# Masks of a whole chunk in one VectorE step, the weights' narrowing spread into the first expert, no warming products in the routing's rounds

## The chip, the cores and the metric

The kernel runs on one core of a Trainium2 chip. The metric is the device time of one execution in microseconds (us). TensorE multiplies matrices into PSUM, VectorE and ScalarE work on PSUM and SBUF, GpSimd on SBUF; SyncE's queue (SP) issues most of the loads, ScalarE's queue and GpSimd issue a few others.

## The reference

Three parts follow each other. First a linear attention with a decay for each channel (4 batches, 8 heads, 768 positions, 48 channels a head), then a mixture of 8 experts in which the highest logits of all pairs choose first and each expert takes 384 tokens, then one more block with squared ReLU that all tokens pass:

```python
for t in range(S):
    state = alpha[:, :, t, :, None] * state + einsum('bhd,bhe->bhde', k[:, :, t], v[:, :, t])
    y[:, :, t] = einsum('bhd,bhde->bhe', q[:, :, t], state)
...
logits = x @ w_gate                       # pairs in falling order; a token is taken once, an expert holds N // 8
out[mask] = np.maximum(x[mask] @ w1[e], 0.0) @ w2[e]
...
r = np.maximum(x @ w_in, 0.0)             # d_model 384, d_ff 2048
return (r * r) @ w_out
```

## The kernel before, in words

**Order.** The order of all instructions is written out by hand: each engine works through its own in the order in which the program issues them, and a DMA queue likewise. Generators (prep, narrow, routing, w_load) give out their instructions a step at a time, where the main loop asks with next().

**Attention** (the loop at L664). There are 24 chunks of 128 positions, six to a batch, two to a unit; 8 heads are 4 pairs, and a pair has one head in rows 0 to 47 and the other in rows 64 to 111. prep (L132) scales q and k of a unit: a backward scan of the alphas (f_t, L144), with which GpSimd multiplies k (L146), a forward scan (b_t, L150) from the reciprocal (L148), and the product with q (L152); the last factors are copied to bend (L149). For a chunk s, state_mm (L227) multiplies k and v, and VectorE adds the sum to the state and scales it with bend (L239, L240). scores (L207) makes the products of q and k for both heads of a pair; ScalarE copies them out (L215) and GpSimd sets what lies in the future to zero (L216). k_tok (L219) transposes k. state_bd (L245) copies the state into a block-diagonal tile, with which y_mm (L250) multiplies q, four products of 128 rows (L256), and adds the masked scores times v (L263). x_out (L273) transposes y and writes it to x_d in DRAM from ScalarE's queue; for the last chunks it comes later, in the routing. logits (L283) and logits_t (L291) give the experts' logits.

**Narrowing** (L167). w_in and w_out come as words of 64 bits. They are loaded in 48 pieces of 256 columns into four buffers, three VectorE steps (L179, L182, L185) turn a piece into 32-bit floats (nb), ScalarE rounds that to a high half (L172) and GpSimd subtracts it for the low half (L173). The main loop asks for two pieces in nearly every chunk; all are done before the experts begin.

**Routing of the first expert** (L448, with kk 0, driven at L713 to L720). A threshold is found digit by digit in six rounds. In a round VectorE compares (above, L414), TensorE counts in 24 products (count, L420), VectorE checks the counts (L489), TensorE spreads the result (L492), VectorE forms the next keys (L505). One late x_out stands in each round. warm(n) (L353) issues n products that nothing reads; they stand after the counts (L482), after the spreading (L493) and further on (L498, L564, L614).

**Experts** (the loop at L971). For each of the 8 experts gemm1 and gemm2 do its two layers over 8 slices, gemm3 and gemm4 the last block over 16 slices. Each product of exact operands takes three matmuls with high and low halves (mm3, L839); the low halves are VectorE's (L878, L913). The next expert's routing runs beside it, a step every few products (tick, L851). There, counts of pairs are formed with cross (L423) and summed over rows by GpSimd (L440). w_load0 (L775) brings the first expert's weights in eight pieces: ScalarE makes the high half (L798), VectorE the low half (L799).

## Time and profile before

| | |
|---|---|
| median of 3 runs | 876.11 us (875.86 to 876.43) |
| span of the profiled execution | 874.0 us |
| PE (TensorE) busy | 811.1 us, 93% |
| DVE (VectorE) busy | 558.7 us, 64% |
| ACT (ScalarE) busy | 398.1 us, 46% |
| POOL (GpSimd) busy | 256.1 us, 29% |
| chain that ended last, shares | PE 69%, DVE 16%, issue 10%, POOL 3%, DMA 2% |

Times in the views below are counted from the start of the span. A group of instructions has its line, engine and operation, what it writes and reads, the shapes and the count, then its busy time, the mean of one in ns, and the idle time of its engine before it with what ended it. A matmul of 32-bit floats counts as two instructions. Attention ends at about 192 us, the first expert's products begin at 239 us.

### The profile page before, as it was taken

To read this page: it belongs to the slowest core of one execution; us is meant where nothing else is said; L and a number is where in the kernel's file an instruction comes from. 1 tells how busy PE (TensorE), PEld (TensorE's weight loads), DVE (VectorE), ACT (ScalarE), POOL (GpSimd) and SP (SyncE) were. 2 spreads that over 40 slices of the span, in tenths; PEclk is the share of its full clock that TensorE was granted. 3 is DMA by queue.
4 is the path that set the end of the run, shared out by engine and by line. 5 is a ranking of instruction groups with operands and counts; after the bars stand their busy time and mean duration, and the time that the engine had idled before them with its cause. 6 is when DMAs were issued, how large, how long until landed. Compare 5 with 4: busy or idle time off the path is not lost.

```text
span 874.0 us, 15157 instructions
## 1 busy us (share of the span) xinstructions
PE 811.1 (93%) x5592; PEld 764.8 (87%) x5592; DVE 558.7 (64%) x1528; ACT 398.1 (46%) x904; POOL 256.1 (29%) x248
## 2 busy tenths in 40 slices
PE   4876878789899999999999999999999999999996
PEld 3755767677599999999999999999999999999996
DVE  8999999983576577567656665765666542432211
ACT  3544546451234553464346245534634553662443
POOL 6687887960111131112201221220131210101001
PEclk9988787895799999999999999999999999999998
DMA  8557768521310230131023004201400332210000
GB/s 302 163 149 203 205 189 214 159 79 55 121 61 1 71 111 20 38 101 62 1 73 100 29 1 136 64 1 55 109 37 1 92 104 59 82 37 28 1 1 28
DMA packets 30219, 73.01 MB, mean 84 GB/s; under 512 B 4384, under 2 KB 8224, under 8 KB 30144
## 3 DMA queue, kind: packets, MB, share of 16 engines
q1 hardware_dynamic: 23616, 57.88, 23.2%
q0 software_dynamic: 3072, 9.44, 3.2%
q10 hardware_dynamic: 3456, 4.72, 1.6%
q8 instruction: 44, 0.72, 0.3%
q14 instruction: 31, 0.25, 0.1%
HBM read 62.58 MB, written 9.44 MB: 82 GB/s over the span
## 4 chain that ended last, share of the span: by engine, by line
PE 69%; DVE 16%; issue 10%; POOL 3%; DMA 2%; SPq 0%; ACT 0%; DVEq 0%; POOLq 0%; ACTq 0%
PE hu_p L842 10%; PE hu_p L844 10%; PE hu_p L843 10%; PE acc L926 7%; PE acc L927 7%; PE acc L922 7%; PE acc L842 3%; PE acc L844 3%; PE acc L843 3%; DVE nb L179 3%; DVE nb L182 3%; DVE nb L185 2%; DVE b_t L150 2%; DVE f_t L144 2%; PE rt_p L420 2%
## 5 line engine op out<-in xcount | busy, mean ns | idle before, releaser
L913 DVE TENSOR_TENSOR gl<-rg,gh 128x384 fp32r<-128x384 f32 x127 | 72.2, 568 | 165.5 <-ACT rg L912 164.7
L910 ACT ACTIVATE rg<-hu_p 128x384 f32<-128x384 f32 x128 | 63.0, 492 | 171.5 <-PE hu_p L844 168.1
L842 PE MATMUL hu_p<-zh,wih 128*128 128x384 f32 x384 | 131.5, 342 | 0.0
L926 PE MATMUL acc<-woh,gh 128*128 128x384 f32 x381 | 130.6, 343 | 0.0
L844 PE MATMUL hu_p<-zl,wih 128*128 128x384 f32 x384 | 129.9, 338 | 0.0
L843 PE MATMUL hu_p<-zh,wil 128*128 128x384 f32 x384 | 128.8, 335 | 0.0
L927 PE MATMUL acc<-wol,gh 128*128 128x384 f32 x381 | 128.6, 338 | 0.0
L440 POOL PARTITION_ALL_REDUCE tot<-ex x48 | 52.3, 1089 | 258.3 <-DVE ex L437 258.3
L922 PE MATMUL acc<-woh,gl 128*128 128x384 f32 x381 | 125.8, 337 | 0.0
L877 ACT ACTIVATE hh<-hu_p 128x384 fp32r<-128x384 f32 x64 | 31.5, 492 | 138.7 <-PE hu_p L844 138.7
L878 DVE SCALAR_TENSOR_TENSOR hl<-hu_p,hh 128x384 fp32r<-128x384 f32 x64 | 35.6, 556 | 63.9 <-ACT hh L877 63.8
L844 PEld LDWEIGHTS hu_p<-zl,wih 128*128 128x128 f32 x384 | 72.1, 188 | 1.2
L843 PEld LDWEIGHTS hu_p<-zh,wil 128*128 128x128 f32 x384 | 72.2, 188 | 0.0
L842 PEld LDWEIGHTS hu_p<-zh,wih 128*128 128x128 f32 x384 | 72.1, 188 | 0.0
L926 PEld LDWEIGHTS acc<-woh,gh 128*128 128x128 f32 x381 | 71.5, 188 | 0.1
L927 PEld LDWEIGHTS acc<-wol,gh 128*128 128x128 f32 x381 | 71.6, 188 | 0.0
L922 PEld LDWEIGHTS acc<-woh,gl 128*128 128x128 f32 x381 | 71.2, 188 | 0.0
L623 POOL DMA_INDIRECT xg<-x_d,ix x24 | 26.4, 1102 | 151.7 <-DVE pe L639 94.2
L911 ACT ACTIVATE gh<-rg 128x384 fp32r<-128x384 f32 x127 | 66.7, 525 | 4.0
L842 PE MATMUL hu_p<-xh,w1h 128*128 128x384 f32 x192 | 66.3, 345 | 0.0
L844 PE MATMUL hu_p<-xl,w1h 128*128 128x384 f32 x192 | 65.7, 342 | 0.0
L948 POOL DMA_INDIRECT out_dram<-ob,ix x24 | 23.7, 988 | 143.0 <-DVE ob L946 139.5
(252 smaller groups left out, 1885.6 us busy)
## 6 DMA issues: line engine op xcount, KB each, us to landing
wraw<-in_w_dram SPq DMA_DIRECT2D x62, 384.0 KB, 3.3
raw<-in_w_in_dram SPq DMA_DIRECT2D x24, 256.0 KB, 3.2
raw<-in_w_out_dram SPq DMA_DIRECT2D x24, 256.0 KB, 3.6
vt<-in_v_dram SPq DMA_DIRECT2D x12, 384.0 KB, 5.4
x_d<-xo ACTq DMA_DIRECT2D x24, 192.0 KB, 2.8
a<-in_al_dram SPq DMA_DIRECT2D x18, 193.7 KB, 4.7
k<-in_k_dram SPq DMA_DIRECT2D x18, 192.0 KB, 5.5
q<-in_q_dram SPq DMA_DIRECT2D x18, 192.0 KB, 6.1
```

The lines of the kernel that those rows point to most:

```text
L440: nc.gpsimd.partition_all_reduce(tot[:, :, :J], ex[:, :, :J], 128, bass_isa.ReduceOp.add)
L842: nc.tensor.matmul(dst, wh, xh, start=first, stop=False)
L843: nc.tensor.matmul(dst, wl, xh, start=False, stop=False)
L844: nc.tensor.matmul(dst, wh, xl, start=False, stop=last)
L877: nc.scalar.activation(hh, hp, AF.Relu)
L878: nc.vector.scalar_tensor_tensor(hl, hp, 0.0, hh.bitcast(FT), op0=OP.max, op1=OP.subtract)
L910: nc.scalar.activation(r, up, AF.Relu)
L911: nc.scalar.activation(gh, r, AF.Square)
L913: nc.vector.tensor_tensor(gl, g, gh.bitcast(FT), op=OP.subtract)
L922: nc.tensor.matmul(acc[j], gl[:, j * 128:(j + 1) * 128], woh[:, f, :], start=False, stop=(f == NF2 - 1))
L926: nc.tensor.matmul(acc[j], gh[:, cs], woh[:, f, :], start=(f == 0), stop=False)
L927: nc.tensor.matmul(acc[j], gh[:, cs], wol[:, f, :], start=False, stop=False)
```

## The change

- **Masks.** scores writes both halves into one PSUM tile of two banks, and one VectorE step, a bitwise and with a constant tile of ones and zeros in all bits, masks and copies them. ScalarE's two copies and GpSimd's two selections of a chunk go.
- **State.** VectorE only adds; the scaling by bend is four ScalarE copies with a scale for each row. The block-diagonal copies go: y_mm has eight products of 48 rows, with outputs that swap halves for odd pairs (side), so that y is copied out in two steps, as are the parts of x.
- **Order.** The q product of a unit comes a chunk later, at the start of the next unit's first chunk, and the loads of v, k, alpha and q are issued apart. Loads of later units are one DMA of 112 rows for each tile instead of two of 48. k is not transposed for the last chunk of a batch.
- **Narrowing.** It goes by 16 tiles, each a slice f of w_in and of w_out of 768 columns together, loaded to a place of its own. In attention it has four steps, the subtraction on VectorE among them, and is asked for beside odd chunks only, twice (once in the last four units). Eight more steps stand in the routing's rounds. From then on a tile is done in halves of 384, three steps with the subtraction on GpSimd, beside the first expert. So 5, 2 and 9 tiles.
- **Routing.** The warming products of the rounds go, and three of six after them. For routing(1) the sum over rows is a TensorE product with ones (total) instead of GpSimd's.
- **First expert's weights.** From the fourth piece on the subtraction is GpSimd's.

```diff
...
 NSL = 3
-NWP = 256
-NWB = 4
+NWP = 768
 BIG = 1.5e38
 WD = 3
+NYT = 4
 S0 = NS - 7
-WR, WC, WA, WB, W0 = 3, 2, 3, 2, 3
+WA, WB, W0 = 3, 2, 3
 T0, T1, T2, T3, XF = 5, 4, 5, 5, 11
...
     pt_ = {}
-    def load(u, ends=(CU * HP,)):
+    def load(u, what="akq", ends=(CU * HP,)):
         i = u % NSL
...
         n0 = 0
         for n1 in ends:
...
-                if u < NSL:
-                    nc.sync.dma_start(t[:, x0:x1], src[u, :, x0:x1])
-                else:
-                    for r in (0, 64):
-                        nc.sync.dma_start(t[r:r + D, x0:x1], src[u, r:r + D, x0:x1])
+                R = slice(0, 128 if u < NSL else R2)
+                nc.sync.dma_start(t[R, x0:x1], src[u, R, x0:x1])
             n0 = n1
     def load_v(u):
-        vs[u] = aw.tile([128, CU, DM], FT, name="vt")
+        vs[u] = aw.tile([128, CU, DM], FT, name="vt", bufs=3)
         nc.sync.dma_start(vs[u], v[u])
...
-    bd = [ap_.tile([128, HP, 128], FT, name=f"bd{i}") for i in range(2)]
-    nc.gpsimd.memset(bd[0], 0.0)
-    nc.gpsimd.memset(bd[1], 0.0)
+    mask = ap_.tile([128, 128], I32, name="mask")
+    yts = [ap_.tile([128, HP, 128], FT, name=f"yt{i}") for i in range(NYT)]
+    for t in yts:
+        nc.gpsimd.memset(t, 0.0)
...
+        nc.scalar.activation(bend[i].rearrange("p c a -> p (c a)")[:, cs], f_t[:, cs, 0], AF.Copy)
         nc.vector.reciprocal(d_b[:, cs, 0], f_t[:, cs, 0])
-        nc.vector.tensor_copy(bend[i].rearrange("p c a -> p (c a)")[:, cs], f_t[:, cs, 0])
...
+    raws, wi, wo = {}, {}, {}
+    def narrow_load(n=1):
+        for _ in range(n):
+            f, o = divmod(len(raws), 2)
+            if f >= NF2:
+                return
+            if not o:
+                raw = consts.tile([128, NWP, 2], U32, name=f"raw{f}", tag=f"w{f}")
+                nc.sync.dma_start(raw[:, :DM].rearrange("p (a b) t -> p a (b t)", a=KD),
+                                  w_in[:, :, f * 128:(f + 1) * 128].bitcast(U32))
+            else:
+                raw = raws[f, 0]
+                nc.sync.dma_start(raw[:, DM:].rearrange("p a t -> p (a t)"), w_out[:, f, :].bitcast(U32))
+            raws[f, o] = raw
+    fine = [None]
+    sub_on = [nc.gpsimd]
     def narrow():
...
+        for f in range(NF2):
+            raw = raws[f, 0]
+            if fine[0] is None:
+                ps = [(aw.tile([128, NWP], U32, name="nb"), slice(0, NWP))]
+            else:
+                ps = [(fine[0].tile([128, DM], U32, name="nb", tag="ob", bufs=3), slice(i * DM, (i + 1) * DM))
+                      for i in range(2)]
+            for t, cs in ps:
+                nc.vector.tensor_scalar(t, raw[:, cs, 1], 3, 0x3FFFFFF8, op0=OP.logical_shift_left,
+                                        op1=OP.bitwise_and)
+            yield False
+            for t, cs in ps:
+                nc.vector.scalar_tensor_tensor(t, raw[:, cs, 1], 0xC0000000, t, op0=OP.bitwise_and,
+                                               op1=OP.bitwise_or)
+            yield False
+            for t, cs in ps:
+                nc.vector.scalar_tensor_tensor(t, raw[:, cs, 0], 29, t, op0=OP.logical_shift_right,
+                                               op1=OP.bitwise_or)
+            w = consts.tile([128, 2, NWP], FR, name=f"w{f}", tag=f"w{f}")
+            for t, cs in ps:
+                nc.scalar.activation(w[:, 0, cs], t.bitcast(FT), AF.Copy)
+            if sub_on[0] is nc.vector:
+                yield False
+            for t, cs in ps:
+                sub_on[0].tensor_tensor(w[:, 1, cs], t.bitcast(FT), w[:, 0, cs].bitcast(FT), op=OP.subtract)
+            wi[f] = w[:, :, :DM].rearrange("p h (a b) -> p h a b", a=KD)
+            wo[f] = w[:, :, DM:]
+            yield True
+    def narrow_upto(n):
+        while len(wo) < n:
+            next(nw)
+    sc_p = pp.tile([128, 2, HP, 128], FT, name="sc_p")
+    y_p = pp.tile([128, 2, HP, 128], FT, name="y_p")
...
                 rr = slice(64 * r, 64 * r + D)
-                nc.tensor.matmul(sc_p[r][:, p, :], ks[i][rr, c, p, :], qs[i][rr, c, p, :], start=True, stop=True)
-        for r in range(2):
-            t = aw.tile([128, HP, 128], FT, name=f"am{r}")
-            nc.scalar.activation(t, sc_p[r], AF.Copy)
-            nc.gpsimd.affine_select(t, t, [[0, HP], [1, C]], OP.is_ge, 0.0, base=0, channel_multiplier=-1)
-            am[s, r] = t
+                nc.tensor.matmul(sc_p[:, r, p, :], ks[i][rr, c, p, :], qs[i][rr, c, p, :], start=True, stop=True)
+        t = aw.tile([128, 2 * HP, 128], FT, name="am")
+        nc.vector.tensor_tensor(t.bitcast(I32), sc_p.rearrange("p r a s -> p (r a) s").bitcast(I32),
+                                mask[:, None, :].to_broadcast([128, 2 * HP, 128]), op=OP.bitwise_and)
+        am[s] = t
     def k_tok(s):
...
         _, j, cn = loc(s + 1)
...
+        src = st_p[R, :, :D]
...
+            nc.vector.tensor_tensor(t0[R], src, st[s - 1][R], op=OP.add)
+            src = t0[R]
+        for p in range(HP):
+            nc.scalar.activation(t[R, p, :], src[:, p, :], AF.Copy, scale=bend[j][R, cn, p:p + 1])
         st[s] = t
-    def state_bd(s):
-        z = bd[(s + 1) % 2]
-        for r in range(2):
-            nc.scalar.activation(z[64 * r:64 * r + D, :, 64 * r:64 * r + D], st[s][64 * r:64 * r + D], AF.Copy)
+    def side(p, r):
+        g = r ^ (p & 1)
+        return slice(64 * g, 64 * g + D)
     def y_mm(s):
...
         f = s % NC == 0
...
         if not f:
             for p in range(HP):
-                nc.tensor.matmul(y_p[:, p, :], bd[s % 2][:, p, :], qs[i][:, c, p, :],
-                                 start=(p == 0), stop=False, skip_group_check=True)
+                for r in range(2):
+                    rr = slice(64 * r, 64 * r + D)
+                    nc.tensor.matmul(y_p[side(p, r), r, p // 2, :], st[s - 1][rr, p, :], qs[i][rr, c, p, :],
+                                     start=(p < 2), stop=False, skip_group_check=True)
...
         for p in range(HP):
...
                 h = 2 * p + r
-                nc.tensor.matmul(y_p[64 * r:64 * r + D, p, :], vs[u][:, c, h * D:(h + 1) * D],
-                                 am[s, r][:, p, :], start=(f and p == 0), stop=True, skip_group_check=True)
+                nc.tensor.matmul(y_p[side(p, r), r, p // 2, :], vs[u][:, c, h * D:(h + 1) * D],
+                                 am[s][:, r * HP + p, :], start=(f and p < 2), stop=True, skip_group_check=True)
...
     before = mr.tile([128, 128], FH, name="before")
...
                                  stop=(c == NS - 1))
-        def cross(self, i):
+        def total(self, i):
+            J = self.J[i]
+            tot = rt_p[:, 200:200 + E * J].rearrange("p (e j) -> p e j", e=E)
+            nc.tensor.matmul(tot, ones, ex[:, :, :J], start=True, stop=True)
+            return tot
+        def cross(self, i, pe):
             J = self.J[i]
...
                                     same[:GP, :E, None].to_broadcast([GP, E, J]), op=OP.mult)
+            if pe:
+                return None
             tot = mw.tile([128, E, 16], FT, name="tot", bufs=1)
...
                             key.count(i, a, b)
-                    if i:
-                        warm(WC)
-                    else:
+                    if not i:
                         x_out(next(late))
...
-                        warm(WR)
                     else:
...
                         nc.tensor.matmul(rt_p[:, 200:200 + E], ones[:J], cg[:J], start=True, stop=True)
-                        warm(6)
+                        warm(3)
                 else:
-                    cp = key.cross(i)
+                    cp = key.cross(i, kk == 1)
                     yield TA
+                    if kk == 1:
+                        cp = key.total(i)
                 dp = mr.tile([128, 1], FT, name="dp", bufs=2)
...
+    nc.vector.tensor_scalar(mask, jp, 0.0, -1.0, op0=OP.is_ge, op1=OP.mult)
+    pr = prep(1)
+    next(pr)
     scores(0)
...
+    narrow_load(2)
     load(2)
...
     NE = NS - 4
-    pr = prep(1)
+    load(3, "a")
     next(pr)
-    next(pr)
+    sub_on[0] = nc.vector
     for s in range(NS):
...
         last = s % NC == NC - 1
-        if c == 1:
-            pr = prep(u + 2) if u + 2 < NU else iter(())
         if not last:
             state_mm(s)
+        if c == 0:
+            next(pr, None)
+            pr = prep(u + 2) if u + 2 < NU else iter(())
         next(pr, None)
...
             scores(s + 1)
-        if not last:
-            state_bd(s)
-        if s + 1 < NS:
+        if s + 1 < NS and (s + 1) % NC != NC - 1:
             k_tok(s + 1)
...
             x_out(s - 1)
-        if s + 2 < NS:
-            next(nw, None)
         if c == 1:
-            next(pr, None)
+            for _ in range(2 if u < 8 else 1):
+                next(nw)
         y_mm(s)
...
             key0.above(0, key0.x, 0, NE)
-        if s + 2 >= NS:
-            next(nw, None)
-        logits_t(s - 1 if s == NS - 1 else s - 2)
-        if 0 < s < NS - 1:
+        if s % 2 == 1 and s > 2:
+            logits_t(s - 2)
+        if s % 2 == 0 and s:
+            logits(s - 2)
             logits(s - 1)
-        if c == CU - 1 and u + NSL < NU:
-            load(u + NSL)
-        if c == CU - 1 and u + 2 < NU:
-            load_v(u + 2)
+        if c == 0:
+            if u + 2 < NU:
+                load_v(u + 2)
+            load(u + NSL, "k")
+        else:
+            load(u + NSL + 1, "a")
+            load(u + NSL, "q")
+        if s % 3 < 2:
+            narrow_load()
         if 2 <= s < 4:
...
+    narrow_load(2 * NF2)
     r0 = routing(0)
     next(r0)
-    for _ in nw:
-        pass
-    for _ in range(len(WIDE) - 1):
+    for n in (2, 1, 2, 2, 1):
         next(r0)
         x_out(next(late))
+        for _ in range(n):
+            next(nw)
         next(r0)
+    sub_on[0] = nc.gpsimd
     att.close()
...
             nc.scalar.activation(fh, got[n], AF.Copy)
-            nc.vector.tensor_tensor(fl, got[n], fh.bitcast(FT), op=OP.subtract)
+            (nc.vector if n < 3 else nc.gpsimd).tensor_tensor(fl, got[n], fh.bitcast(FT), op=OP.subtract)
             if len(got) < len(todo):
...
         up = hu()
-        cs = slice(f * 128, (f + 1) * 128)
+        narrow_upto(f + 1)
         for kd in range(KD):
-            mm3(up, (wih[:, kd, cs], wil[:, kd, cs]), (zh[:, kd, :], zl[:, kd, :]), kd == 0, kd == KD - 1)
+            mm3(up, (wi[f][:, 0, kd, :], wi[f][:, 1, kd, :]), (zh[:, kd, :], zl[:, kd, :]), kd == 0, kd == KD - 1)
             tick()
...
                 next(wl[0], None)
+                for _ in range(1 + f % 2):
+                    next(nw, None)
             hn = gemm1(kk, f + 1) if f + 1 < NF1 else None
...
                 h = gemm1(kk + 1, 0)
+            if kk == 0:
+                next(nw, None)
+                next(nw, None)
             if more and f == XF + 3:
...
```

## Rows read from the trace of the kernel before

**Rows 1.** Windows in us: length; PE, PEld, DVE, ACT, POOL busy (count); PEclk; DMA share; GB/s.
```profile
12.00:19.00 7.00, 6.55 (x54) 4.97 (x54) 6.96 (x8) 3.13 (x7) 6.61 (x4) 1.00 1.04 405
120.00:140.00 20.00, 16.46 (x189) 14.18 (x189) 19.93 (x26) 11.05 (x27) 16.97 (x12) 0.79 0.72 196
```

**Rows 2.** The chain that ended last, 140 to 180: start us, us, what.
```profile
143.60 2.21 DVE b_t L150
...
147.58 0.41 DVE nb L179 x2
147.99 0.67 DVE nb L182 x2
...
152.00 2.94 DVE nb L179 x2
...
158.66 2.29 DVE b_t L150
```

**Rows 3.** Groups of VectorE's instructions by shape, 19 to 192: busy us, mean ns, idle.
```profile
L179 DVE TENSOR_SCALAR nb<-raw 128x256 uint32<-128x256 uint32 x47 | 34.0, 761 | 3.6 <-POOL wil L173 2.3 <-POOL wol L173 1.2
L182 DVE SCALAR_TENSOR_TENSOR nb<-raw,nb 128x256 uint32<-128x256 uint32 x46 | 27.6, 639 | 0.0
L185 DVE SCALAR_TENSOR_TENSOR nb<-raw,nb 128x256 uint32<-128x256 uint32 x46 | 26.9, 624 | 0.0
L144 DVE TENSOR_TENSOR_SCAN f_t<-a,d_f 128x1032 f32<-128x1032 f32 x10 | 23.5, 2349 | 0.0
L150 DVE TENSOR_TENSOR_SCAN b_t<-a,d_b 128x1032 f32<-128x1032 f32 x10 | 22.9, 2295 | 0.0
L152 DVE TENSOR_TENSOR q<-q,b_t 128x1024 f32<-128x1024 f32 x11 | 13.6, 1236 | 0.0
...
L240 DVE TENSOR_TENSOR st<-st,be 112x192 f32<-112x192 f32 x16 | 6.6, 412 | 0.6
L239 DVE TENSOR_TENSOR st<-st_p,st 112x192 f32<-112x192 f32 x16 | 5.5, 341 | 0.6 <-PE st_p L231 0.6
```

**Rows 4.** The same of GpSimd.
```profile
L146 POOL TENSOR_TENSOR k<-k,f_t 128x1024 f32<-128x1024 f32 x11 | 27.4, 2491 | 7.0 <-DVE f_t L144 7.0
```

**Rows 5.** The same of ScalarE.
```profile
L248 ACT ACTIVATE bd<-st 48x192 f32<-48x192 f32 x39 | 14.0, 360 | 42.9 <-DVE st L240 29.9 <-DVE st L242 12.7
...
L271 ACT ACTIVATE yt<-y_p 128x512 f32<-128x512 f32 x18 | 10.6, 589 | 4.7 <-PE y_p L263 4.5
```

**Rows 6.** TensorE's timeline at the end of attention: start us, us, engine, line, operation.
```profile
181.03 1.93 PE L256 MATMUL y_p<-q,bd 128*128 128x128 f32 x8
...
184.75 0.56 PE L231 MATMUL st_p<-vt,kt 128*48 128x48 f32 x16
...
189.12 1.16 PE L256 MATMUL st_p<-q,bd 128*128 128x128 f32 x8
```

**Rows 7.** TensorE's timeline in one round of the routing.
```profile
209.68 0.18 PE L492 MATMUL rt_p<-cm,ones 31*128 31x1 f16 x1
...
210.73 0.95 PE L276 MATMUL kt_p<-ident,a 112*128 112x112 f32 x4
211.61 1.76 PE L420 MATMUL rt_p<-oh,m 128*31 128x8 f16 x24
...
214.06 0.18 PE L492 MATMUL rt_p<-cm,ones 31*128 31x1 f16 x1
```

**Rows 8.** VectorE's timeline in that round.
```profile
210.18 0.62 DVE L414 TENSOR_TENSOR m<-xn,jc 128x372 f16<-128x372 f16 x2
...
213.41 0.15 DVE L489 TENSOR_SCALAR_CACHE_REDUCE cg<-rt_p 31x8 f16<-31x8 f32 x1 [2.31 <-PE rt_p L420]
```

**Rows 9.** Windows of the routing and the first expert.
```profile
208.00:212.00 4.00, 4.00 (x31) 2.64 (x31) 1.29 (x7) 0.28 (x1) 0.20 (x1) 0.50 0.16 53
239.00:291.00 52.00, 51.63 (x290) 50.86 (x290) 34.68 (x114) 19.73 (x40) 9.36 (x8) 0.95 0.10 37
```

**Rows 10.** VectorE's groups by shape, 225 to 262.
```profile
L799 DVE TENSOR_TENSOR w1l<-wraw,w1h 128x768 fp32r<-128x768 f32 x3 | 2.9, 955 | 0.0
```

More of the change, by code (lines that the diff above doesn't have):

```diff
@@ L68 @@
     L = consts.tile([128, NS, E], FT)
-    wih = consts.tile([128, KD, F2], FR)
-    wil = consts.tile([128, KD, F2], FR)
-    woh = consts.tile([128, NF2, DM], FR)
-    wol = consts.tile([128, NF2, DM], FR)
     mr = ctx.enter_context(tc.tile_pool(name="route", bufs=1))
@@ L93 @@
     pt_ = {}
-    def load(u, ends=(CU * HP,)):
+    def load(u, what="akq", ends=(CU * HP,)):
         i = u % NSL
+        if u >= NU:
+            return
+        ts = {"a": (as_[i], al), "k": (ks[i].rearrange("p c a s -> p (c a s)"), k),
+              "q": (qs[i].rearrange("p c a s -> p (c a s)"), q)}
         n0 = 0
         for n1 in ends:
-            for t, src in ((as_[i], al), (ks[i].rearrange("p c a s -> p (c a s)"), k),
-                           (qs[i].rearrange("p c a s -> p (c a s)"), q)):
+            for t, src in (ts[w] for w in what):
                 w = src.shape[-1] // (CU * HP)
@@ L128 @@
     load_v(1)
-    nc.sync.dma_start(wgs, wg)
+    for b in range(2):
+        for r in range(2):
+            nc.sync.dma_start(wgs[64 * r:64 * r + 64].rearrange("p (k b) e -> p b k e", b=2)[:, b],
+                              wg[64 * (r ^ b):64 * (r ^ b) + 64].rearrange("p (k b) e -> p b k e", b=2)[:, b])
     nc.gpsimd.iota(jp, pattern=[[1, 128]], base=0, channel_multiplier=-1)
@@ L153, in prep @@
         yield
-    wq = []
-    for h_, l_, src in ((wih, wil, w_in), (woh, wol, w_out)):
-        h2, l2, s2 = (t.rearrange("p a b -> p (a b)") for t in (h_, l_, src))
-        wq += [(h2[:, j:j + NWP], l2[:, j:j + NWP], s2[:, j:j + NWP]) for j in range(0, h2.shape[1], NWP)]
-    raws = []
-    def narrow_load():
-        if len(raws) < len(wq):
-            raw = aw.tile([128, NWP, 2], U32, name="raw", bufs=NWB)
-            nc.sync.dma_start(raw.rearrange("p a b -> p (a b)"), wq[len(raws)][2].bitcast(U32))
-            raws.append(raw)
@@ L195 @@
     xt_p = pp.tile([128, HP, 128], FT, name="xt_p")
-    lg_p = pp.tile([128, 4, 128], FT, name="lg_p")
-    lt_p = pp.tile([128, 4, 128], FT, name="lt_p")
-    y_ps = (y_p, st_p)
+    lg_p = rt_p
+    lt_p = lg_p[:, 256:].rearrange("p (j g) -> p j g", j=2)
     xt_ps = (xt_p, kt_p)
@@ L268, in y_mm @@
         else:
-            yt[s] = aw.tile([128, HP, 128], FT, name="yt")
-        for ps in ([slice(0, HP)] if s < NS - 1 else [slice(0, HP // 2), slice(HP // 2, HP)]):
-            nc.scalar.activation(yt[s][:, ps], y_p[:, ps], AF.Copy)
+            yt[s] = yts[s % NYT]
+        for g in range(2):
+            rr = slice(64 * g, 64 * g + D)
+            nc.scalar.activation(yt[s][rr].rearrange("p (k b) s -> p b k s", b=2),
+                                 y_p[rr, ::(1, -1)[g], :2], AF.Copy)
     def x_out(s):
@@ L277, in x_out @@
         t = aw.tile([128, H, D], FT, name="xo")
-        nc.scalar.activation(t, xt_p.rearrange("p a (r d) -> p (a r) d", r=2)[:, :, :D], AF.Copy)
+        for b in range(2):
+            nc.scalar.activation(t.rearrange("p (k b r) d -> p b k r d", b=2, r=2)[:, b],
+                                 xt_p.rearrange("p (k b) (r d) -> p b k r d", b=2, r=2)[:, b, :, ::(1, -1)[b], :D],
+                                 AF.Copy)
         nc.scalar.dma_start(x_d[s * C:(s + 1) * C, :], t.rearrange("p h d -> p (h d)"))
@@ L648 @@
             pass
-    for t in (y_p, st_p, lg_p):
-        nc.scalar.activation(t, bd[0], AF.Copy)
+    nc.scalar.activation(st_p, yts[0], AF.Copy)
+    nc.scalar.activation(lg_p, yts[0].rearrange("p a s -> p (a s)"), AF.Copy)
     nc.vector.tensor_scalar(ident, jp, 0.0, None, op0=OP.is_equal)
+    nc.vector.tensor_scalar(mask, jp, 0.0, -1.0, op0=OP.is_ge, op1=OP.mult)
+    pr = prep(1)
+    next(pr)
     scores(0)
-    for _ in range(NWB):
-        narrow_load()
+    narrow_load(2)
     load(2)
```

75 lines of the change are left out of this document (25 added, 50 removed).

## The prediction

> **What bounds the kernel now.** I read the windows first, then the chain of waits, then the groups by line. The windows cut the span in three. Until the last chunk at about 192 us (attention), VectorE is the full engine: 19.93 of 20 us in 120:140, with TensorE at 16.46 and a granted clock of 0.79 [rows 1]. From 192 to 239 (routing of the first expert) TensorE's chain sets the time, at clock 0.50 although the engine is always busy [rows 9]. From 239 on TensorE is full: 51.63 of 52 us in 239:291 [rows 9]. The rest runs so to the end, and the change leaves experts 1 to 7 as they are.
>
> In attention the chain of waits is almost only VectorE. One unit (two chunks) goes from scan to scan: 143.60 to 158.66, 15.06 us [rows 2]. The same narrowing step costs 0.41 us for two pieces at 147.58 and 2.94 us at 152.00, when GpSimd is at its masks and subtractions [rows 2]. On average the three steps of a piece of 256 cost 0.761, 0.639 and 0.624 us, 88.5 us in the stage [rows 3]; alone they would be 0.205, 0.335 and about 0.335 [rows 2].
>
> **Attention, VectorE, per unit after the change.** Stays: the two scans 2.35 + 2.30, the q product 1.24 (it only moves by a chunk), two state additions 0.68 [rows 3]. Leaves: the four pieces' 12 narrowing steps, 8.1 us at the means, the state's multiplication, 2 x 0.41 [rows 3], and the small copy of the alphas, which I don't count. Comes: two masks and two narrowing steps. A mask is one operation on 128x1024, which no row shows. Nearest is the q product, same size and one result per element, 1.24; the other end is a scan at 2.35 [rows 3]. I take 1.24, since it is a product of the same kind: 2.48 a unit. A narrowing tile now has 768 columns and four steps: 3 x 0.205, twice 3 x 0.335 [rows 2] and the subtraction, 0.955 [rows 10]: 3.6 us, or 1.8 for two steps. They may be taken at the price without GpSimd, whose masks and subtractions are gone; only the k product is left there, 2.49 a unit [rows 4]. Sum: 2.35 + 2.30 + 1.24 + 0.68 + 2.48 + 1.8 = 10.9 us.
>
> That GpSimd slows the narrowing is shown by [rows 2]. The Trainium skill (SBUF — State Buffer, section Who interferes with whom) says that VectorE contends with GpSimd only in instructions with two SBUF inputs or in a two-port mode; a mask, with one input in PSUM, wouldn't. By that the mask stays at its price beside the k product; no row here shows such a pair.
>
> **Attention, the other engines.** TensorE's chunk, back to back at full clock, runs from 184.75 to 189.12: 4.37 us, without the transposes of x [rows 6], which take 0.88 at half clock (210.73 to 211.61) [rows 7]. So 5.2 us a chunk with small things, 10.4 a unit: nearly as much as VectorE. The state's products become eight of 48 rows instead of four of 128; I take them at the old 1.1 us [rows 6] (one of them half as dear would give 0.5 a chunk, which isn't the bound). If the clock stays at 0.79, 10.4 becomes 13.1. In 12:19, with TensorE at 6.55 of 7 us, the clock was 1.00 [rows 1], and shorter idle times speak for it. I take 11.7 a unit, between VectorE's 10.9 and TensorE at 0.79, nearer to the first.
> ScalarE loses four mask copies and four copies of 0.36 a unit and gets eight scaled copies of the state (at most 0.36 each, the row with 192 columns [rows 5]) and a second copy of y for each chunk (0.589 [rows 5]): it was at 11.05 of 20 us [rows 1] and stays under 9 of 11.7. Its scaled copies are queued ahead of the k transposes' copy, which the next state product waits for a whole chunk later: hidden at up to 2 us.
> DMA: a unit brings about 2.7 MB (three tiles of 112 rows of 4 KB, v, 1.3 narrowing tiles, x out): 230 GB/s at 11.7 us. 0.72 busy at 196 GB/s is 272 GB/s when full, and whole tiles reached 405 [rows 1]. So hidden, with little to spare; a late alpha would stop the scan and all behind it on VectorE. On SP's queue the q load now waits for the unit's last y product, and a narrowing load and the next v stand behind it; each has over a chunk until its use.
> Ten units prepare a later one: 10 x (15.06 - 11.7) = **33.6 us gained**. Bounds: 41.6 at 10.9, 19.6 at 13.1 (with the mask at the scan's price VectorE would come to the same 13.1). Start and last two units I take at nothing: the mask constant and two early masks are added, one narrowing step of the first chunks leaves, and the last chunks are TensorE's already [rows 6]; 4 us either way.
>
> **Routing.** A round takes 4.38 us, from 209.68 to 214.06 [rows 7]. Products that nothing reads fill about 0.9 of it ahead of the transposes at 210.73, and 0.7 after the count, which ends near 213.3 [rows 7]. The transposes (0.88) cover VectorE's x and keys: those end at 210.80 [rows 8], 1.1 after the round's start. Without the products a round is 0.1 + 1.0 + 1.7 for the count + 0.4 for VectorE's check and its way back = 3.2. Five rounds: 6 us. The narrowing steps put there (8 of 0.6 to 1.0) stand ahead of that check on VectorE; it idled 2.31 us there [rows 8], now some 1.2, so that rounds with two steps overrun by 0.2 to 0.6: 1.1 back. Three fewer warming products at the end: 0.6. **5.5 us gained**, bounds 2 to 8.
>
> The clock is 0.50 in 208:212 with the warming products in and TensorE full [rows 9], so their removal can't lower it there. The Trainium skill (TensorE: Matmul & The Clock Gate, section Why this matters for your kernels) warns of idle gaps between bursts, after which the array runs at its lower clock. By that the warming products left after the rounds would start slow and the gain would shrink by about 2.4 us to 3.
>
> **Expert 0.** Nine of 16 narrowing tiles are now done here, in halves of 384, beside a full TensorE. VectorE was busy 34.68 us in 239:291 [rows 9]. Five subtractions of 0.955 go to GpSimd (-4.8) [rows 10]; narrowing comes: 18 halves at 0.3 + 0.5 + 0.5 = 23 us (scaled from [rows 2]). That is 53 of 52 us. At the contended means [rows 3] it is 18 x 3.04 = 55, or 85 of 52. GpSimd has 18 subtractions of 0.93 and five of 1.87 (scaled from the k product [rows 4]), 26 us. VectorE's lag reaches TensorE through the low halves of h and g, which have about 3 us of slack, and through a new wait: the sum over rows of routing(1) becomes a product on TensorE, and all that is queued behind it there waits for VectorE's ex. Bounds: 0 (the uncontended sum within the slack) and 20 (two thirds of the contended excess). I take **9 us lost**, nearer to the uncontended end, since GpSimd is busy half of the time.
>
> **Sum.** -33.6 - 5.5 + 9 = -30. The profiled execution spans 874.0; the median, 876.1, lies 2.1 above it, and what lies around the span doesn't change. 874.0 - 30 + 2.1 = **846 us**.
>
> **Rivals.**
> 1. Contention in expert 0 takes the gain: narrowing there at the contended prices, 20 us instead of 9: 857. For it: [rows 2], a step seven times as dear; against: GpSimd half as busy. The Trainium skill's rule above would have it so, since all narrowing steps have two SBUF inputs or are of the fast kind.
> 2. Attention stays at 13.1 a unit, since TensorE and VectorE wait for each other in turn (scores need the mask before, masks the scores) or the mask costs a scan: 860.
> 3. All hides well: 10.9 a unit, 7 in routing, 3 lost: 876.1 - 41.6 - 7 + 3 = 830.
> 4. Slower: TensorE at its lower clock throughout attention, as the routing stage has it when always busy [rows 9]. A product group of 1.1 us took 1.9 there (181.03 against 189.12 [rows 6]), 1.7 times; 1.7 x 10.4 = 17.7 a unit, 10 x 2.6 = 26 lost, 876.1 + 26 - 5.5 + 9 = 906. It decides from a unit of 14.7 on, a mean clock below 0.71. Against: 0.79 with many idle times, 1.00 when dense [rows 1].
> 5. The change doesn't unload VectorE, because the narrowing that was taken away is only moved: 7 of 16 tiles stay ahead of the experts, and of 5 of them 18 us in attention against 88.5 [rows 3]. I give it nothing.
>
> **How the numbers follow.** Forecast 0.58 (836 to 853), rival 1 0.18, rival 2 0.12, rival 3 0.08, rival 4 0.04. The range takes in rivals 1, 2 and most of 3: 829 to 864. About 0.2% is what a measurement can tell here. Only rival 4 is slower; 0.01 for no change: faster 0.95, same 0.01, slower 0.04.
>
> **What would show it.** Scan to scan 11 to 12.5 us a unit; narrowing steps near 0.6, 1.0, 1.0; the mask at 1.2; attention's end near 157 instead of 192; rounds of 3.2 to 3.6; TensorE idle in expert 0 before products that wait for VectorE, 5 to 12 us, none in expert 1. I am wrong if the unit stays above 13, if TensorE waits for DMA in attention, or if expert 0 grows by over 20.

## The result, and the profile after

The changed kernel takes **861.92 us** (860.25 to 863.32) where the kernel before takes 876.2: a ratio of 0.9837 [0.9823, 0.985], 14.3 us gained instead of 30. The profiled execution spans 860.3 us against 874.0. Three marks divide both spans: the first warming product behind attention (L358 before, L381 after) and the first product of an expert (hu_p from xh).

| stretch | before | after | difference | forecast |
|---|---|---|---|---|
| attention, to the warming product | 191.88 | 155.74 | -36.1 | -33.6 |
| routing, to the first expert product | 47.14 | 42.42 | -4.7 | -5.5 |
| the experts, to the end | 635.0 | 662.1 | +27.1 | +9 |

The marks on TensorE's timeline (start us, us, engine, line, operation), first before, then after:

```profile
191.88 0.49 PE L358 MATMUL y_p<-jc 128*128 128x384 f16 x2
239.02 0.69 PE L842 MATMUL hu_p<-xh,w1h 128*128 128x384 f32 x1
```

```profile
155.74 0.80 PE L381 MATMUL y_p<-jc 128*128 128x384 f16 x2 [0.76 <-ACT yt L290]
198.16 0.69 PE L881 MATMUL hu_p<-xh,w1h 128*128 128x384 f32 x1
```

Two terms came out, the third is three times the forecast. The loss lies in expert 0: from its first product to expert 1's it is 107.3 us where it was 80.2, and from there to expert 2's 78.9 where it was 78.8.

The windows of after (us: length; PE, PEld, DVE, ACT, POOL busy and count; granted clock; DMA share; GB/s), which answer [rows 1, 9]:

```profile
80.00:100.00 20.00, 15.71 (x262) 12.59 (x260) 18.77 (x20) 11.23 (x31) 4.06 (x2) 0.97 0.92 276
120.00:140.00 20.00, 17.79 (x247) 13.97 (x240) 17.49 (x18) 9.94 (x26) 4.34 (x2) 0.77 0.71 227
198.00:300.00 102.00, 82.50 (x435) 77.49 (x434) 79.73 (x220) 40.08 (x89) 30.26 (x26) 0.92 0.13 44
300.00:340.00 40.00, 40.00 (x237) 39.11 (x236) 28.29 (x93) 17.08 (x42) 9.94 (x12) 1.00 0.15 45
```

In 198:300, 52 us of which were full before [rows 9], TensorE now works 82.5 of 102 us. Yet VectorE isn't full either: 79.73. A busy share alone doesn't explain it; the waits do. TensorE is idle for 19.5 us of this window, and 17.3 of it is put down to VectorE. Its longest waits there (engine, line waited for, us in total, times, longest):

```profile
PE rt_p L449 <- DVE ex L466: 8.3, 3, 5.2
PE rt_p L457 <- DVE m L437: 5.8, 3, 3.1
PE acc L883 <- DVE hl L917: 2.6, 1, 2.6
```

The first two are products of routing(1), queued among the expert's own. The first is the new sum with ones (total). What VectorE did before its longest wait, and what GpSimd did meanwhile (timeline: start, us, engine, line; first VectorE, then GpSimd, then TensorE):

```profile
202.58 1.81 DVE L414 TENSOR_SCALAR kb<-vm 128x24 int32<-128x24 int32 x1
204.31 0.35 DVE L416 TENSOR_TENSOR eq<-L,vm 128x192 f32<-128x192 f32 x1
204.58 1.82 DVE L417 TENSOR_TENSOR kb<-kb,vm 128x24 int32<-128x24 int32 x1
...
212.43 4.52 DVE L404 TENSOR_SCALAR dg<-kb 128x24 int32<-128x24 int32 x7
```

```profile
202.52 1.84 POOL L838 TENSOR_TENSOR w2l<-rg,w2h 128x768 fp32r<-128x768 f32 x1 [7.10 <-ACT w2h L837]
204.31 2.04 POOL L838 TENSOR_TENSOR w1l<-rg,w1h 128x768 fp32r<-128x768 f32 x1
211.21 1.99 POOL L200 TENSOR_TENSOR w<-nb,w 128x384 fp32r<-128x384 f32 x2 [4.86 <-ACT w L196]
213.15 1.83 POOL L838 TENSOR_TENSOR w2l<-wraw,w2h 128x768 fp32r<-128x768 f32 x1
214.94 1.82 POOL L838 TENSOR_TENSOR w1l<-wraw,w1h 128x768 fp32r<-128x768 f32 x1
```

```profile
212.57 0.45 PE L883 MATMUL acc<-hl,w2h 128*128 128x384 f32 x1
218.22 0.26 PE L449 MATMUL rt_p<-ex,ones 128*128 128x120 f16 x1 [5.21 <-DVE ex L466]
218.25 0.67 PE L881 MATMUL acc<-hh,w2h 128*128 128x384 f32 x1
218.72 0.52 PE L882 MATMUL acc<-hh,w2l 128*128 128x384 f32 x1
...
221.44 0.33 PE L882 MATMUL hu_p<-xh,w1l 128*128 128x384 f32 x1
```

An integer step on 24 columns takes 1.81 us and ends at 204.39, with GpSimd's subtraction (204.36). Seven such steps take 4.52 and end at 216.95, with the last subtraction (216.76). TensorE stands 5.21 us behind them, and then runs its products at 0.52 instead of 0.33 us for 3 us: the granted clock is 0.98 in 213:218, where it was idle, and 0.68 in 218:223.

### The profile page after: what moved, and what is told of

Same layout as the page of the kernel before. It is cut to its first block, busy times and chain, and to the rows that moved or that the text cites. A ratio compares the mean times of both kernels' runs of the same rounds, so it can differ in the third digit from the quotient of the medians.

```text
span 860.3 us, 15100 instructions
## 1 busy us (share of the span) xinstructions
PE 792.0 (92%) x5715; PEld 744.6 (87%) x5715; DVE 542.3 (63%) x1457; ACT 391.4 (45%) x934; POOL 152.3 (18%) x169
## 4 chain that ended last, share of the span: by engine, by line
PE 64%; issue 9%; DVE 6%; POOL 1%; ACT 1%; DMA 0%; POOLq 0%; DVEq 0%
PE hu_p L881 10%; PE hu_p L883 10%; PE hu_p L882 10%; PE acc L965 7%; PE acc L966 6%; PE acc L961 6%; PE acc L881 3%; PE acc L883 3%; PE acc L882 3%; PE rt_p L443 1%; DVE nb L192 1%; PE rt_p L457 1%; PE xq_p L874 1%; POOL out_dram L987 1%; DVE nb L184 1%
## 5 line engine op out<-in xcount | busy, mean ns | idle before, releaser
L881 PE MATMUL hu_p<-zh,w 128*128 128x384 f32 x384 | 133.3, 347 | 2.2 <-ACT zh L930 2.2
L883 PE MATMUL hu_p<-zl,w 128*128 128x384 f32 x384 | 131.4, 342 | 0.0
L965 PE MATMUL acc<-w,gh 128*128 128x384 f32 x381 | 131.2, 344 | 0.0
L882 PE MATMUL hu_p<-zh,w 128*128 128x384 f32 x384 | 130.3, 339 | 0.0
L966 PE MATMUL acc<-w,gh 128*128 128x384 f32 x381 | 129.2, 339 | 0.0
L961 PE MATMUL acc<-w,gl 128*128 128x384 f32 x381 | 126.2, 338 | 0.0
L881 PEld LDWEIGHTS hu_p<-zh,w 128*128 128x128 f32 x384 | 73.2, 191 | 4.6 <-ACT zh L930 2.5
L883 PEld LDWEIGHTS hu_p<-zl,w 128*128 128x128 f32 x384 | 73.3, 191 | 1.4 <-DVE zl L931 0.3
L882 PEld LDWEIGHTS hu_p<-zh,w 128*128 128x128 f32 x384 | 73.2, 191 | 0.0
L965 PEld LDWEIGHTS acc<-w,gh 128*128 128x128 f32 x381 | 71.8, 189 | 0.1
L966 PEld LDWEIGHTS acc<-w,gh 128*128 128x128 f32 x381 | 71.9, 189 | 0.0
L961 PEld LDWEIGHTS acc<-w,gl 128*128 128x128 f32 x381 | 71.7, 189 | 0.0
L883 PE MATMUL acc<-hl,w2h 128*128 128x384 f32 x192 | 65.0, 338 | 2.6 <-DVE hl L917 2.6
L881 PE MATMUL acc<-hh,w2h 128*128 128x384 f32 x192 | 65.9, 343 | 0.0
```

Source lines behind the costliest of these rows:

```text
L881: nc.tensor.matmul(dst, wh, xh, start=first, stop=False)
L882: nc.tensor.matmul(dst, wl, xh, start=False, stop=False)
L883: nc.tensor.matmul(dst, wh, xl, start=False, stop=last)
L961: nc.tensor.matmul(acc[j], gl[:, j * 128:(j + 1) * 128], wo[f][:, 0, :], start=False, stop=(f == NF2 - 1))
L965: nc.tensor.matmul(acc[j], gh[:, cs], wo[f][:, 0, :], start=(f == 0), stop=False)
L966: nc.tensor.matmul(acc[j], gh[:, cs], wo[f][:, 1, :], start=False, stop=False)
```

## The experiments

Attention's length differs by up to 4.7 us between profiles whose edits touch neither it nor the routing (first expert product at 195.7 to 200.4); no run shows why. So the experiments on expert 0 are read by the **expert time**, from the first expert product to the end of the profiled span: 662.1 after, and 662.8 and 662.4 in the two kernels below whose edits lie ahead of it. Differences under 1 us in it say nothing.

| kernel | median us | expert time |
|---|---|---|
| before | 876.2 | 635.0 |
| after | 861.92 | 662.1 |
| e1, first expert's weights: all subtractions on VectorE | 859.41 | 658.8 |
| e8, the tiles' subtractions on VectorE too | 849.26 | 649.7 |
| f3, e8 and an idle subtraction on GpSimd | 857.78 | 655.6 |
| e3, nine tiles' narrowing left out | 838.23 | 640.9 |
| g1, e3 and e1 | 835.28 | 634.7 |
| e2, after with routing(1)'s sum on GpSimd | 917.5 | 718.1 |
| f1, e8 with that sum on GpSimd | 852.66 | 655.3 |
| e6, after, narrowing one product earlier | 858.91 | 659.2 |
| f2, e8, the same | 852.24 | 651.6 |
| f4, f1 and f2 | 858.45 | 656.3 |
| e7, after, two and one steps in turn | 857.4 | 656.2 |
| g2, e8, the same | 863.86 | 663.4 |
| e4, warming products back | 869.18 | 662.8 |
| e5, each mask twice | 884.91 | 662.4 |

### How much is narrowing (e3, g1)

```diff
     fine[0] = mw
+    for f in range(len(wo), NF2):
+        wi[f], wo[f] = wi[f - 7], wo[f - 7]
+    nw = iter(())
```

> The nine narrowing tiles of the first expert are left out (products use earlier tiles). What remains against the kernel before is the gain of attention and routing and the cost of the other two edits in the first expert. Rival T: all of the loss of 27 us goes, 834 to 837. Theory Q: the subtractions of the first expert's weights on GpSimd still hold VectorE's integer steps up, so that 4 to 9 us of the loss stay, 839 to 845.

838.23 lies between the two expectations; 21.2 us of expert time go (662.1 to 640.9). g1 adds e1's edit:

```diff
-            (nc.vector if n < 3 else nc.gpsimd).tensor_tensor(fl, got[n], ...)
+            nc.vector.tensor_tensor(fl, got[n], ...)
```

> Leaves out the narrowing of the last nine hidden tiles (the products read the parts of earlier tiles) and has all the subtractions of the first expert's weights on VectorE. From the first expert product to the end the kernel before took 634.9 us, the changed one 662.1, the one without the nine tiles 640.9, the one with only the weights' subtractions on VectorE 658.8. Theory A (the weights' subtractions on GpSimd slow VectorE whether or not it narrows beside them, and the two prices add): 637 to 638.5. Theory B (they only cost where VectorE is full of narrowing): 640 to 642, and what is left of the loss belongs to the second routing's sum.

634.7, below both expectations and equal to the kernel before (635.0). So the whole loss is accounted for by the nine tiles and by five subtractions of the first expert's weights on GpSimd; routing(1)'s new sum, without them, costs no more than GpSimd's sum did before. (ScalarE's rounding of the nine tiles goes with them. With all subtractions on VectorE, in e8 below, 10.1 of TensorE's 12.4 us of waiting are put down to VectorE and 2.1 to ScalarE.) With the weights' subtractions on VectorE and no narrowing, TensorE is full again (window of g1):

```profile
198.00:300.00 102.00, 101.84 (x596) 98.42 (x595) 68.48 (x237) 45.01 (x102) 10.43 (x13) 0.99 0.20 62
```

### Which engine subtracts (e1, e8, f3)

> All eight subtractions of the first expert's weights go back to VectorE. Theory Q (queue): in the first expert VectorE is not short of time (79.7 of 102 us in 198 to 300 of the changed kernel); TensorE stalls since single VectorE steps stand behind a whole GpSimd subtraction (a step on 24 integers takes 1.8 us instead of 0.17) and all behind them waits. Then some 9 us of such waits go, 4.8 us of subtractions come: 4 to 8 us faster than the changed kernel, 854 to 858. Rival T (throughput): VectorE simply has too much to do; 4.8 us more make it 0 to 5 us slower, 862 to 867. Rival W (the new wait on TensorE for the sum over rows) expects no change.

859.41 lies between theories Q and T: 3.3 us of expert time, less than I gave the contention; without narrowing the same edit is worth 6.2 (e3 to g1). e8 also leaves out the line that hands the tiles' subtractions to GpSimd:

```diff
-    sub_on[0] = nc.gpsimd
```

> All subtractions of the first expert (its weights' and the narrowing's) are VectorE's, GpSimd has none. Theory C (contention): VectorE's steps lose some 15 us in 198 to 300 beside GpSimd's subtractions (24-column integer steps at 0.6 to 1.0 us instead of 0.17, first narrowing steps at 0.55 instead of 0.31, and others); these go, and 13 us of subtractions come, which need no GpSimd to hand back a buffer: 0 to 8 us faster than the changed kernel. Rival T: 13 us more of VectorE work make it 8 to 13 us slower, 870 to 875.

849.26 us, 12.4 us of expert time gained, more than expected, although 18 subtractions came to VectorE and made it busier (windows as above, of e8):

```profile
198.00:300.00 102.00, 89.59 (x509) 84.17 (x510) 86.59 (x271) 47.04 (x106) 7.11 (x10) 0.99 0.17 54
```

The same seven steps (e8, VectorE's timeline), and the first narrowing step of a half in both kernels (groups: busy us, mean ns; after, then e8):

```profile
210.44 0.66 DVE L404 TENSOR_SCALAR dg<-kb 128x24 int32<-128x24 int32 x7
```

```profile
L184 DVE TENSOR_SCALAR nb<-raw 128x384 uint32<-128x384 uint32 x18 | 9.3, 551 | 2.8 <-POOL w L200 2.8
L404 DVE TENSOR_SCALAR dg<-kb 128x24 int32<-128x24 int32 x9 | 4.9, 595 | 0.0
```

```profile
L184 DVE TENSOR_SCALAR nb<-raw 128x384 uint32<-128x384 uint32 x18 | 5.6, 353 | 0.0
L404 DVE TENSOR_SCALAR dg<-kb 128x24 int32<-128x24 int32 x16 | 1.7, 171 | 0.0
```

Over all VectorE groups of one form, count in after times the difference of the means, after spends 14.2 us more on the same steps: 3.6 in L184 and 10.6 in small steps of the routing. Against e1 after spends 8.8 more: so most of these longer steps go with the weights' five subtractions, which cost only 3.3 us, and the other 5.4 with the tiles', which cost 9.1. Longer steps on VectorE are not yet time lost on TensorE.

Was contention (steps that last longer beside GpSimd's) the price, or VectorE's waits for GpSimd's results (2.8 us ahead of L184 above)? f3 puts idle subtractions beside e8:

```diff
                 sub_on[0].tensor_tensor(w[:, 1, cs], ...)
+                if fine[0] is not None:
+                    wf = w[:, 0, cs].bitcast(FT)
+                    for a, b in ((0, 256), (256, DM)):
+                        nc.gpsimd.tensor_tensor(jp.bitcast(BF)[:, :b - a], wf[:, a:b], wf[:, a:b], op=OP.subtract)
```

> The subtractions of expert 0 on VectorE, and beside each of the nine tiles' subtractions one of the same size on GpSimd whose result nobody reads and whose inputs stay alive anyway. It adds GpSimd's traffic and no wait on GpSimd. Theory C (VectorE's steps are slowed while GpSimd reads two inputs): most of the 12.7 us come back, 856 to 865, with steps of 24 columns that take 1.8 us again. Theory W (in the changed kernel VectorE waited for GpSimd to give buffers back): 848 to 851.

857.78: 5.9 us of expert time come back without anyone waiting for GpSimd, as theory C has it. So GpSimd's subtractions can cost VectorE and TensorE time by running beside them alone. It doesn't take apart the 9.1 us between e1 and e8, though: theory C's sign is missing (no small step reached 1.8 us; the 24-column steps of L404 above took 0.60 at most, and GpSimd's instructions last 0.68 us here instead of 1.0 to 2.0), and what was slowed are mostly VectorE's own subtractions (554 to 751 ns, 3.5 us), which e1 doesn't have there. How much of the 9.1 is contention and how much buffers given back late stays open.

### Who sums (e2, f1)

```diff
-                    cp = key.cross(i, kk == 1)
+                    cp = key.cross(i, False)
...
-                    if kk == 1:
-                        cp = key.total(i)
```

> The sum over rows in routing(1) goes back to GpSimd, so that TensorE has no product that waits for VectorE's ex. Rival W: the 8.3 us that TensorE waited there are the loss; 6 to 8 us faster than the changed kernel, 854 to 856. Theory Q: VectorE is late in any case, the wait moves to the next counts and the low halves, and the reduction is one more GpSimd step for VectorE to stand behind: between 1 us faster and 4 us slower, 861 to 866. Rival T: no change.

917.5, far from every expectation. GpSimd's timeline in e2:

```profile
208.71 1.99 POOL L200 TENSOR_TENSOR w<-nb,w 128x384 fp32r<-128x384 f32 x2 [4.86 <-ACT w L196]
216.78 1.04 POOL L471 PARTITION_ALL_REDUCE tot<-ex  x1 [6.08 <-issue]
224.69 1.79 POOL L836 TENSOR_TENSOR w2l<-wraw,w2h 128x768 fp32r<-128x768 f32 x1 [6.86 <-issue]
...
236.25 1.04 POOL L471 PARTITION_ALL_REDUCE tot<-ex  x1 [6.05 <-issue]
244.39 1.83 POOL L836 TENSOR_TENSOR w2l<-wraw,w2h 128x768 fp32r<-128x768 f32 x1 [7.09 <-issue]
```

Between a subtraction and a sum it stands 5.7 to 7.1 us, waiting for nothing that the profile shows, both ways and in eight of the nine changes (the ninth, 6.73 us, is put down to VectorE): 51.2 us of it between 198 and 300 (30.2 ahead of the sums, 21.0 ahead of subtractions). In f1, where the subtractions are VectorE's, it has nothing to change between.

> The subtractions of expert 0 on VectorE (that alone gave 849.3 us) and the second routing's sum back on GpSimd (that alone gave 917.5). Theory S, that the 56 us of that run were GpSimd's stops of 6 to 7 us at every change between a subtraction and a sum over the partitions: with no subtractions beside the sums there is almost nothing to change between, so 845 to 853. Theory M, that the sum on GpSimd is itself the price (its way from VectorE over GpSimd to TensorE, once a round): most of the 56 us stay, 885 to 905.

852.66, the first theory: the changes were the 56 us, or nearly all of them. Against e8 the sum on GpSimd still loses 5.6 us of expert time, so TensorE's sum is the better one.

### Order in VectorE's queue (e6, e7, f2, f4, g2)

e6 and f2 ask for the two steps of narrowing of gemm3's slice one product earlier, e7 and g2 for fewer:

```diff
+            if kk == 0:
+                next(nw, None)
+                next(nw, None)
             if f + 1 < NF2:
                 gn = gemm3(z, f + 1)
...
             if kk == 0:
-                next(nw, None)
-                next(nw, None)
```

```diff
             if kk == 0:
-                next(nw, None)
-                next(nw, None)
+                for _ in range(2 - f % 2):
+                    next(nw, None)
```

> In the first expert's last block the two narrowing steps of a slice are asked for before its gemm3, not after, so that they stand ahead of the low half gl (which waits for TensorE and ScalarE) on VectorE. Theory O (order): they now run while gl isn't ready, and routing steps behind them come earlier: 3 to 8 us faster than the changed kernel, 854 to 859. Rival T (throughput: 27 us of VectorE work come back as 27 us wherever they stand): within 2 us of 862.

> In the first expert's last block two narrowing steps stand beside even slices and one beside odd ones, so that the first step of a tile no longer follows the last one of the tile before. Theory B (buffers): there are three buffers for halves, two per tile; the first step of the next tile waits on VectorE until GpSimd has subtracted, and the routing's steps stand behind it, 2 to 3 us for each of five tiles: 6 to 12 us faster than the changed kernel, 850 to 856. Rival T: the same work for VectorE, within 2 us of 862.

2.9 and 5.9 us of expert time, just short of the 3 to 8 and the 6 to 12: where the steps stand counts a little while GpSimd is beside them. In e7 VectorE's 2.8 us of waiting for buffers ahead of L184 are gone; that this alone gave the 5.9 isn't shown. With VectorE's subtractions an earlier place gives nothing:

> The subtractions of expert 0 on VectorE, and the two steps of narrowing of each hidden tile asked for one matrix product earlier. With GpSimd in the subtractions the earlier place alone gave 3.0 us. Theory Q (what is left is VectorE's queue: a product's own step waits behind a narrowing step): the same gain again, 845 to 847.5. Theory L (VectorE is simply full, 86.6 of 102 us busy between 198 and 300 us, and order inside its queue changes nothing): 848.5 to 850.

> All three: the subtractions of expert 0 on VectorE, the second routing's sum on GpSimd, narrowing asked for one product earlier. If the sum on GpSimd takes VectorE's and TensorE's work off without a new wait (theory S) and the order counts (theory Q), 842 to 848; if neither, 849 to 853; if the sum is the price (theory M), 885 to 905.

f2's expert time is 1.9 above e8's, f4's 1.0 above f1's; in the profiles, the rest of the difference lies ahead of the first expert product, in the spread named above.

> The subtractions of expert 0 on VectorE, and the hidden tiles' steps of narrowing asked for as two and one in turn in place of two and two, so that they last over more products. With GpSimd in the subtractions the spacing alone gave 5.9 us from the first expert product to the end (656.2 of 662.1); VectorE's subtractions alone gave 649.7. Theory Q (what is left is products' own steps behind narrowing steps in VectorE's queue): 645 to 648. Theory L (VectorE is full, and the work only moves): 649 to 652.

863.86, outside both. I had forgotten the date by which the work is due: with the subtraction as a fourth step of its own, nine tiles are 36 steps, and with fewer asked for, two of the last slices of expert 0's last block came to tiles that weren't ready, 9.5 us of waiting (TensorE's timeline in g2; expert 1 begins at 305.43):

```profile
299.23 0.69 PE L880 MATMUL hu_p<-zh,w 128*128 128x384 f32 x1 [5.91 <-ACT w L196]
```

### Routing and attention (e4, e5)

e4 puts the warming products of the rounds back, behind the counts and behind the spreading:

```diff
-                    if not i:
+                    if i:
+                        warm(2)
+                    else:
                         x_out(next(late))
...
                         nc.tensor.matmul(rt_p[:, 200:201], ones[:J], cm[:J], start=True, stop=True)
+                        warm(3)
```

> The warming products of the routing's rounds come back, nothing else. If they were on the path, as the prediction had it, a round is longer by 1.0 to 1.3 us: 5 to 6.5 us slower than the changed kernel, 867 to 868.5. If the narrowing steps on VectorE set the rounds, 1 to 3 us slower. If the rounds without them made the array's clock rise later, it is faster than the changed kernel by 1 us or more.

869.18, 7.3 slower; the routing stretch grows by 5.2 us (42.4 to 47.7), as the first case has it, and a round takes 4.38 again instead of 3.04 to 3.39, at a granted clock of 0.50 in both (TensorE's timeline in e4):

```profile
175.33 0.18 PE L523 MATMUL rt_p<-cm,ones 31*128 31x1 f16 x1
179.71 0.18 PE L523 MATMUL rt_p<-cm,ones 31*128 31x1 f16 x1
```

They were on the path. e5 does each mask a second time:

```diff
                                 mask[:, None, :].to_broadcast([128, 2 * HP, 128]), op=OP.bitwise_and)
+        nc.vector.tensor_tensor(t.bitcast(I32), sc_p..., mask..., op=OP.bitwise_and)
         am[s] = t
```

> Each mask step is issued twice (the second writes the same once more). It asks what bounds attention after the change. If VectorE does, as the prediction had it, 24 steps of 1.2 us come on top: 25 to 29 us slower than the changed kernel, 887 to 891. If TensorE or a wait between the two sets the chunk, 6 to 15 us slower, 868 to 877.

23.0 us slower, short of the 25 to 29 that VectorE as the bound was to give and far above the 6 to 15. The first expert product comes 24.3 us later than after's (222.48 against 198.16), of 24 x 1.22 = 29 us added: attention is still set by VectorE for the most part, though its windows show 17.49 to 18.77 of 20 us. No run takes attention's edits apart, so what the mask, the state's copies, the order and the narrowing gave each isn't shown.

## Why the prediction was right or wrong

**Attention, -33.6, measured -36.1: right, with misses that in part cancel, which is luck.** The groups that answer [rows 3, 4] (after, 19 to 156 us):

```profile
L149 DVE TENSOR_TENSOR_SCAN b_t<-a,d_b 128x1032 f32<-128x1032 f32 x11 | 32.8, 2980 | 0.4
L232 DVE TENSOR_TENSOR am<-sc_p,mask 128x1024 int32<-128x1024 int32 x23 | 27.6, 1200 | 3.6 <-PE sc_p L230 3.6
...
L188 DVE SCALAR_TENSOR_TENSOR nb<-raw,nb 128x768 uint32<-128x768 uint32 x5 | 4.8, 956 | 0.1
L192 DVE SCALAR_TENSOR_TENSOR nb<-raw,nb 128x768 uint32<-128x768 uint32 x5 | 4.7, 943 | 0.0
L184 DVE TENSOR_SCALAR nb<-raw 128x768 uint32<-128x768 uint32 x5 | 2.7, 544 | 0.0
```

The mask took 1.20 (1.24 taken), narrowing 0.54, 0.96, 0.94 (0.6, 1.0, 1.0). The scan b_t rose from 2.295 to 2.98, since the k product of GpSimd now runs beside it; I had the contention gone. Before, that product stood beside the narrowing step of 2.94 us at 152.00 for which [rows 2] was cited (I put the masks and subtractions there; GpSimd's timeline, before):

```profile
152.56 2.23 POOL L146 TENSOR_TENSOR k<-k,f_t 128x1024 f32<-128x1024 f32 x1
```

From the first full scan to the last, ten units took 113.7 us (20.76 to 134.45), but the first of them took 6.19 and the other nine 11.94 on average, where I said 11.7 (VectorE's timeline, after):

```profile
20.76 2.31 DVE L149 TENSOR_TENSOR_SCAN b_t<-a,d_b 128x1032 f32<-128x1032 f32 x1
26.95 4.03 DVE L149 TENSOR_TENSOR_SCAN b_t<-a,d_b 128x1032 f32<-128x1032 f32 x1
```

Before they took 157.95 (15.93 to 173.88), 15.8 each: the one unit of [rows 2] that I took for all, 15.06, is like most (eight of ten took 14.98 to 15.61), but two early ones took 16.25 and 19.45. That is 44.3 us gained between the scans. Start and end, which I took at nothing, 4 either way, lost 8.1 of it: the first full scan comes 4.8 later, and from the last one to the warming product it is 21.3 instead of 18.0. The products of y with the state cost 0.66 where I took the old 1.1, which isn't the bound (after, TensorE's timeline, against [rows 6]):

```profile
142.85 1.16 PE L230 MATMUL sc_p<-q,k 48*128 48x128 f32 x16
143.94 0.60 PE L239 MATMUL kt_p<-ident,k 112*128 112x112 f32 x4
144.47 0.66 PE L274 MATMUL y_p<-q,st 48*48 48x128 f32 x16
```

**Rival 4 (slower by the clock)** fell: 0.97 in 80:100, 0.77 in 120:140, units of 10.8 to 12.3 us in both. Rival 2 (attention at 13.1 a unit, 860 us) is near the result by its number alone: units took 11.94 and the mask 1.20.

**Routing, -5.5, measured -4.7: right.** Rounds after, answering [rows 7]:

```profile
172.54 0.16 PE L521 MATMUL rt_p<-cm,ones 31*128 31x1 f16 x1 [0.26 <-DVE cg L518]
175.58 0.16 PE L521 MATMUL rt_p<-cm,ones 31*128 31x1 f16 x1 [0.26 <-DVE cg L518]
178.97 0.16 PE L521 MATMUL rt_p<-cm,ones 31*128 31x1 f16 x1 [0.59 <-DVE cg L518]
```

3.04 and 3.39, for 3.2 with overruns of 0.2 to 0.6. The 0.6 for three warming products less behind the rounds didn't come: from the last round's product to the expert's first it is 16.2 us before and 16.1 after. Nor did the products left there start slower: the granted clock goes from 0.60 to 1.00 in 224:232 before and from 0.61 to 1.00 in 184:192 after.

**Expert 0, 9 lost, measured 27.1: the term that was mis-sized**, beyond even its bound of 20, and the growth by over 20 that the prediction gave as a sign of being wrong. The mechanism, VectorE's lag reaching TensorE, was named, and so was the new wait; three things went wrong in the size.
- The sum of VectorE's work already stood at 53 of 52 us uncontended, and I let slack absorb it (about 3 us, for which I gave no row); the step "nearer to the uncontended end, since GpSimd is busy half of the time" then left 9. The runs give the parts on one path: narrowing with all its subtractions on VectorE costs 15.0 (e8 less g1); handing the tiles' subtractions to GpSimd takes 10 us of work off VectorE (18 x 0.554) and costs 9.1 more (e1 less e8); the weights' cost 3.3 (after less e1): 27.4. What the 53 would cost with no GpSimd beside them, no run shows.
- The contention was priced on the narrowing steps alone. In after only 3.6 of its 14.2 us fell there; the routing's integer steps on 24 columns, 0.17 us each, which I didn't count at all, took 7.1, and TensorE's queue waits directly behind them.
- The five subtractions given to GpSimd were booked as 4.8 us saved. They cost 3.3.

Part of the price isn't idleness. In 198:300 TensorE works 82.50 us on 435 instructions in after, 101.84 on 596 in g1: at g1's 0.171 us the 435 would take 74.3. By that estimate (the mix of shapes is not quite the same) 8 us of after's loss are a lower clock behind idle times (0.92 against 0.99) and 19.5 are idle; in e1, 8 and 16.2; in e8, 2.6 and 12.4. So more than half of the 9.1 us between e1 and e8 is clock. The prediction had no term for it.

The Trainium skill (SBUF — State Buffer, section Who interferes with whom) says that where VectorE and GpSimd contend (VectorE in a two-port mode, or with two SBUF inputs beside a GpSimd read) the one that issues first holds the shared ports for a whole instruction, and the other stands still. The rows agree, 1.81 us beside 1.84.

Rival 1, worth 18% to me, put all of the loss, 20 us, on contention. What came with GpSimd's subtractions is 12.4 of the 27.1; the 15.0 of e8 come without them.

## What to carry to other kernels

Work moved off a full engine to a stage where another engine is the bound has to fit there with what already queues on it: price the small steps behind which the bound engine waits, not only the moved ones. Giving a helper engine part of the work can cost more than doing it: with all of the narrowing's steps and the weights' subtractions on VectorE (e8, 849.26 us, a ratio of 0.9693 [0.9674, 0.9712]) the kernel is better than both before and after. And take a unit's length from all units, first to last, not from one.

## What the runs showed of the hardware

- VectorE's short integer steps lasted until the GpSimd subtraction beside them ended: 1.81 us for 0.18. The scan, with two inputs in SBUF, went from 2.30 to 2.95 beside a product of 2.18, and took 2.31 where the product was about to end (65.16 against 65.31). The mask, which reads PSUM and one SBUF tile, was not slowed: 1.19 to 1.23 in all of its 24.
- GpSimd stood still for 5.7 to 7.1 us at changes between elementwise work and a sum over the partitions (e2), eight times between 198 and 300 us. The Trainium skill (GPSIMD Engine Reference, section 2.1 Instruction dispatch) gives some 6 us for the first call of freshly loaded code, with no instruction to be seen; the size agrees, and here it is paid again and again; that code is loaded at these changes no run shows.
- Eight products of 48 rows (after, L274) took 0.66 us where four of 128 rows (before, L256) took 1.07, both at a granted clock of 1.00; at 0.50 it was 1.11 and 1.94.
